# An attention turn in another order: four score tiles, a pair's values in one run, three score tiles

## The chip, the cores and the metric

The kernel runs on one core of a Trainium2 chip. The core has a tensor engine (PE), whose weight loads are a row of their own in the profile (PEld), a vector engine (DVE), a scalar engine (ACT), GpSimd (POOL) and queues that issue DMA transfers (SP among them). Each engine takes its instructions in program order, and semaphores hold an instruction back until what it needs is there. The metric is device microseconds of one execution, the median of several runs.

## The reference

Attention over 4 batches of 12 heads, 448 positions and 64 columns per head, and behind it two gated MLPs over the 1792 tokens that come out:

```python
q_n, k_n = (rmsnorm(q, g_q), rmsnorm(k, g_k))      # each row / its rms, times g
scores = scale * np.matmul(q_n, k_n.transpose(0, 1, 3, 2))
scores = scores - np.max(scores, axis=-1, keepdims=True)
attn = np.exp(scores)
attn = attn / (np.sum(attn, axis=-1, keepdims=True) + 1e-09)
out = np.matmul(attn, v)                           # (4, 12, 448, 64)
x = out.transpose(0, 2, 1, 3).reshape(1792, 768)
x = (x @ w_a * (x @ w_b)) @ w_out                  # 768 -> 1536 -> 768
x = (sigmoid(x @ w_gate) * (x @ w_val)) @ w_out2   # the same sizes
```

All inputs and the result are 32-bit floats.

## The kernel before

Attention takes the 48 heads as 24 pairs; the first 320 us are theirs, and the MLPs behind them are not touched. The two heads of a pair lie in the two halves of the 128 partitions. The 448 positions are 384 (three blocks of 128) and a remainder of 64. For each pair the work goes through these steps, each a small function in the code:

- `load`, `load_r`, `load_v` fetch q and k, the remainder rows of a whole batch, and v. `squares` (POOL), `mean` (DVE), `rsqrt` (ACT), `newton` (DVE) make the factor 1/rms of each row, `scale` (POOL) multiplies by it.
- `t_tr` transposes q (four PE transposes) and k (five); `q_hi`, `k_hi` (ACT) round the result to a short float (QH, KH), `q_lo`, `k_lo` (DVE) keep what the rounding lost (QL, KL).
- `s` makes a score tile as three products, KH by QH, KH by QL, KL by QH. The rows of queries make seven tiles of 128 x 448: tiles t and t+4 belong to the two heads and are made together, in the two row halves of the array (`s(i, 0)`, `s(i, 1)`, `s(i, 2)`, two tiles each); tile 3 holds the remainder queries of both heads and uses the full array. `top` (DVE) takes the row maximum, `exp` (ACT) the exponential with the row sum. Four banks of PSUM hold scores.
- `x_tr` transposes the exponentials back, by blocks j of 128 keys, j = 3 the remainder; `x_out` copies the result from PSUM to SBUF, z = 0 by ACT, z = 1 by DVE. Three banks of PSUM hold what PE transposes, `t_tr` and the row sums included.
- `pv` multiplies values and exponentials, two heads for each block j, the heads in the two column halves of the array. The remainder block uses quarters of the array: 64 rows of a head's keys by 64 columns.
- `rsum`, `rsum_tr`, `rsum_post` turn the sums into reciprocals, transpose them and write them to DRAM (`dr`); `rsum_get` reads them back spread over partitions (`rs`, three DMAs), `norm` (DVE) multiplies `pv` by `rs` into `xs`, and `put` stores it. `early`, `early_hi`, `early_lo` prepare, for six of the last pairs, what the first MLP starts with: `early_lo` is a POOL subtraction over 896 columns.

The order on every engine is written out by hand. `begin`, `turns` and `end` are tables of entries (step, offset, arguments); `turns` runs once for each pair i from 1 to 22, and an entry with offset o works on pair i + o. The program order on each engine is the order in which the entries come. In a turn of the kernel before, the products of values come at four places (`pv(-2, 3)`, `pv(-1, 0)`, `pv(-1, 1)`, `pv(-1, 2)`), and score tiles at four places between transposes.

Of the kernel before, what the change touches and what calls it, by code (L numbers as in the profile page):

```python
# [23 lines left out]
def attention_then_two_gated_mlps(  # L24
# [93 lines left out]
    def attention():  # L118
# [22 lines left out]

        qrem = fx.tile([P, P], F32, name="qrem")
# [40 lines left out]
        def squares(i):  # L183
# [4 lines left out]
            r = rem[i // NP][0][:, :, i % NP]  # L188
# [32 lines left out]
        def scale(i, n):  # L221
# [45 lines left out]
        def k_hi(i):  # L267
            d = st[i]
            KH, KL = (qk.tile([P, S], F32R, tag=n, name=n) for n in ("KH", "KL"))
# [4 lines left out]
            nc.scalar.activation(out=KH, in_=d["T", 1][:, 0:S], func=AF.Copy, scale=G)  # L274
# [5 lines left out]
        def k_lo(i):  # L280
# [3 lines left out]
            nc.vector.scalar_tensor_tensor(out=KL, in0=kt, scalar=G, in1=f32(KH), op0=ALU.mult, op1=ALU.subtract)  # L284

        def s(i, t):
# [18 lines left out]
        def exp(i, t):  # L305
            d = st[i]
            e = pp.tile([P, S], F32, tag="P", name="P")
# [3 lines left out]
            d["P"][t] = e  # L311

        def x_tr(i, j, z):
# [3 lines left out]
            if j < R:  # L317
                if z == 0:
                    out7 = tr.rearrange("p (b x) -> p b x", x=64)[:, 0:8:7, :]
                    nc.tensor.transpose(out7, p[3][:, P * j:P * j + P], ident)  # L320
                o = 0 if z else 64
                for c in range(3):
                    nc.tensor.transpose(tr[:, o + P * c:o + P * c + P], p[4 * z + c][:, P * j:P * j + P], ident)  # L323
                return
            for m, a, perm in ((128, 4, swap), (64, 0, ident)):
                nc.tensor.transpose(tr[0:m, 0:P], p[3][:, S - m:S], perm)
                for c in range(3):
                    nc.tensor.transpose(tr[0:m, 64 + P * c:64 + P * c + P], p[a + c][:, S - m:S], ident)
# [12 lines left out]
        def pv(i, j):  # L341
            d = st[i]
            b, hp = divmod(i, NP)
            if j == 0:
                d["pv"] = ps_v.tile([P, S], F32, tag="pv", name="pv")
            for h in range(2):
                e = slice(64 * h, 64 * h + 64)
                if j < R:
                    w, x = d["v"][:, R * h + j], d["pt"][j][:, S * h:S * h + S]
                else:  # L350
                    w, x = rem[b][1][e, hp], d["pt"][j][e, 0:S]
                nc.tensor.matmul(d["pv"][e], w, x, start=(j == 0), stop=(j == R), skip_group_check=True)  # L352
# [77 lines left out]
        def mlp(i, n):  # L430
# [10 lines left out]
            (exp, 0, 0), (q_lo, 1), (rsqrt, 2), (k_hi, 1), (top, 0, 4), (s, 0, 3), (exp, 0, 4), (newton, 2),
            (squares, 3), (top, 0, 1), (exp, 0, 1), (k_lo, 1), (s, 0, 2), (scale, 2, 1),
            (top, 0, 5), (exp, 0, 5), (top, 0, 3), (exp, 0, 3), (scale, 2, 2), (top, 0, 2),
            (top, 0, 6), (t_tr, 2, 1), (scale, 2, 0), (t_tr, 2, 0), (exp, 0, 2), (mean, 3),
            (s, 1, 0), (load, 4), (k_hi, 2), (k_lo, 2), (top, 1, 0), (q_hi, 2),
            (load_r, 3), (squares, 4), (q_lo, 2), (x_tr, 0, 0, 0),
# [3 lines left out]
            (top, 0, 4), (exp, -1, 6), (rsqrt, 2), (early_hi, -1), (s, 0, 1), (x_tr, -1, 0, 1), (top, 0, 1),  # L450
            (exp, 0, 0), (x_out, -1, 0, 0), (exp, 0, 4), (pv, -2, 3), (load_v, 1), (norm, -2),
            (s, 0, 3), (put, -2), (early_lo, -1), (early, 0), (top, 0, 5), (exp, 0, 1), (newton, 2), (x_tr, -1, 1, 0),
            (x_out, -1, 0, 1), (x_tr, -1, 1, 1), (scale, 2, 1), (top, 0, 3), (x_out, -1, 1, 0),
            (exp, 0, 5), (pv, -1, 0), (s, 0, 2), (x_tr, -1, 2, 0), (scale, 2, 2),
            (rsum, -1), (x_out, -1, 1, 1), (top, 0, 2), (rsum_tr, -1),
            (exp, 0, 3), (scale, 2, 0), (top, 0, 6), (x_tr, -1, 2, 1), (x_out, -1, 2, 0),
            (rsum_post, -1), (exp, 0, 2), (pv, -1, 1), (x_out, -1, 2, 1),
            (load, 4), (load_r, 3), (t_tr, 2, 1), (x_tr, -1, 3, 0), (t_tr, 2, 0),
            (mean, 3), (s, 1, 0), (k_hi, 2), (q_hi, 2), (k_lo, 2), (squares, 4),
            (x_out, -1, 3, 0), (q_lo, 2), (pv, -1, 2), (x_tr, 0, 0, 0), (top, 1, 0),  # L460
            (rsum_get, -1),
# [3 lines left out]
            (exp, -2, 6), (top, -1, 4), (s, -1, 1), (x_tr, -2, 0, 1), (rsum, -2), (exp, -1, 0), (top, -1, 1),  # L465
            (s, -1, 3), (x_out, -2, 0, 0), (exp, -1, 4), (x_out, -2, 0, 1),
            (pv, -3, 3), (exp, -1, 1), (top, -1, 5), (rsum_tr, -2),
            (norm, -3), (x_tr, -2, 1, 0), (top, -1, 3), (rsum_post, -2), (x_tr, -2, 1, 1), (s, -1, 2),
# [7 lines left out]
            (x_tr, -1, 0, 1), (pv, -2, 3), (rsum, -1), (x_out, -1, 1, 0), (x_out, -1, 0, 1), (decode, -1, 4),
            (decode, -1, 5), (decode, -1, 6), (decode, -1, 7),
            (decode, -1, 8), (mlp, -1, 0), (stage, -1, "A21", 0), (rsum_tr, -1), (x_tr, -1, 1, 1), (mlp, -1, 1),
            (rsum_post, -1), (mlp, -1, 2), (x_out, -1, 1, 1), (decode, -1, 9), (norm, -2),
            (mlp, -1, 3), (stage, -1, "A21", 1), (x_tr, -1, 2, 0), (x_tr, -1, 2, 1),  # L480
            (mlp, -1, 4), (pv, -1, 0), (x_out, -1, 2, 0), (x_out, -1, 2, 1), (mlp, -1, 5),
            (mlp, -1, 6), (stage, -1, "A21", 2),
            (pv, -1, 1), (x_tr, -1, 3, 0), (mlp, -1, 7), (x_out, -1, 3, 0), (mlp, -1, 8),
            (rsum_get, -1), (mlp, -1, 9), (pv, -1, 2), (stage, -1, "A11", 0),
            (mlp, -1, 10), (mlp, -1, 11), (put, -2),
            (mlp, -1, 12), (pv, -1, 3), (mlp, -1, 13), (stage, -1, "A11", 1), (norm, -1), (mlp, -1, 14), (put, -1),
# [758 lines left out]
```

## Time and profile before

| | |
|---|---|
| time, median of 3 runs | 1297.03 us (1294.79 to 1297.15) |
| the profiled execution | 1292.24 us |
| its span in the trace | 1290.5 us, so 1.74 us lie around it |
| granted PE clock, mean | 0.989 |
| PE busy in the span | 1241.7 us (96%) |
| DVE, ACT, POOL busy | 938.9 us, 658.0 us, 169.5 us |

The profile is of one execution. Busy time of PE counts a matmul from its start to its modelled end, and matmuls overlap, so the duration in a row of PE is longer than the time until the next row starts; the distance between starts is what a group of matmuls costs. The attention part is the first ten of the forty slices of the span: PE is busy 9 tenths of each slice but the first, POOL 4 or 5 tenths, ACT 6 or 7, DVE 6 or 7.

### The profile page before, as it was taken

To read this page: it belongs to the slowest core of one execution; us is meant where nothing else is said; L and a number is where in the kernel's file an instruction comes from. 1 tells how busy PE (TensorE), PEld (TensorE's weight loads), DVE (VectorE), ACT (ScalarE), POOL (GpSimd) and SP (SyncE) were. 2 spreads that over 40 slices of the span, in tenths; PEclk is the share of its full clock that TensorE was granted. 3 is DMA by queue.
4 is the path that set the end of the run, shared out by engine and by line. 5 is a ranking of instruction groups with operands and counts; after the bars stand their busy time and mean duration, and the time that the engine had idled before them with its cause. 6 is when DMAs were issued, how large, how long until landed. Compare 5 with 4: busy or idle time off the path is not lost.

```text
span 1290.5 us, 18247 instructions
## 1 busy us (share of the span) xinstructions
PE 1241.7 (96%) x6486; PEld 1020.0 (79%) x6486; DVE 938.9 (73%) x1617; ACT 658.0 (51%) x1267; POOL 169.5 (13%) x200
## 2 busy tenths in 40 slices
PE   5999999999979999999999998989999999999997
PEld 3555555555658888888888887878888888899997
DVE  7676767676797778777567688976778777558583
ACT  4666666766454353343444645653454453444543
POOL 4454445540000000000002022000000000000000
PEclk9999999999989999999999999989999999999999
DMA  4333233323914455555486563413556556487573
GB/s 110 88 93 100 80 101 120 120 75 109 312 45 137 139 171 193 165 175 194 147 299 195 169 224 109 139 61 125 173 159 195 165 164 202 157 289 244 179 250 119
DMA packets 142026, 203.01 MB, mean 157 GB/s; under 512 B 23240, under 2 KB 116592, under 8 KB 141936
## 3 DMA queue, kind: packets, MB, share of 16 engines
q1 hardware_dynamic: 140816, 201.27, 48.9%
q8 instruction: 51, 0.84, 0.3%
q10 hardware_dynamic: 1120, 0.59, 0.2%
q14 instruction: 39, 0.32, 0.1%
HBM read 147.46 MB, written 54.35 MB: 156 GB/s over the span
## 4 chain that ended last, share of the span: by engine, by line
PE 59%; DVE 8%; ACT 3%; issue 2%; DMA 1%; ACTq 0%; SPq 0%; DVEq 0%
PE mm L865 41%; PE mm L1127 9%; PE mm L1117 8%; DVE xl L554 2%; DVE wl L554 1%; ACT gh L1034 1%; DVE d L1004 1%; DVE gl L554 1%; DVE al L778 1%; DVE u L1022 0%; DVE d L624 0%; DVE raw L620 0%; DVE u L778 0%; DVE d L700 0%; DMA u<-gd 0%
## 5 line engine op out<-in xcount | busy, mean ns | idle before, releaser
L865 PE MATMUL mm<-xh,wh 128*128 128x512 f32 (+1 forms) x1008 | 371.6, 369 | 11.0 <-ACT u L917 4.1
L865 PE MATMUL mm<-xl,wh 128*128 128x512 f32 (+1 forms) x1008 | 371.8, 369 | 4.7 <-DVE xl L554 4.7
L865 PE MATMUL mm<-xh,wl 128*128 128x512 f32 (+1 forms) x1008 | 372.4, 369 | 0.0
L554 DVE TENSOR_TENSOR wl<-d,wh 128x384 fp32r<-128x384 f32 x252 | 143.7, 571 | 153.7 <-ACT wh L712 93.5
L865 PEld LDWEIGHTS mm<-xh,wh 128*128 128x128 f32 x1008 | 191.4, 190 | 38.9 <-ACT u L917 5.1
L865 PEld LDWEIGHTS mm<-xl,wh 128*128 128x128 f32 x1008 | 191.1, 190 | 30.0 <-DVE xl L554 7.1
L865 PEld LDWEIGHTS mm<-xh,wl 128*128 128x128 f32 x1008 | 191.0, 189 | 21.6 <-DVE wl L554 0.3
L712 ACT CAST wh<-d 128x384 fp32r<-128x384 f32 x168 | 85.9, 512 | 168.1 <-DVE d L700 142.1
L301 DVE TENSOR_REDUCE nm<-s 128x1 f32<-128x448 f32 x168 | 99.8, 618 | 32.1 <-PE s L295 31.9
L1007 ACT CAST wh<-d 128x384 fp32r<-128x384 f32 x84 | 43.2, 514 | 149.9 <-DVE d L1004 54.3
L308 ACT ACTIVATE P<-s,nm 128x448 f32<-128x448 f32 x168 | 106.6, 636 | 15.9 <-DVE nm L301 15.1
L617 ACT ACTIVATE d<-raw 128x384 f32<-128x384 f32 x136 | 75.8, 558 | 72.9 <-DMA raw<-in_moe_w_gate_dram 15.0
L1127 PE MATMUL mm<-wh,gh 128*128 128x384 f32 x294 | 98.8, 336 | 0.5 <-ACT ah L1150 0.3
L1127 PE MATMUL mm<-wl,gh 128*128 128x384 f32 x294 | 98.6, 335 | 0.0
L1127 PE MATMUL mm<-wh,gl 128*128 128x384 f32 x294 | 98.5, 335 | 0.0
L1117 PE MATMUL mm<-gh,wh 128*128 128x512 f32 x252 | 92.5, 367 | 5.1 <-ACT ah L1150 4.4
L1117 PE MATMUL mm<-gl,wh 128*128 128x512 f32 x252 | 93.2, 370 | 0.0
L1117 PE MATMUL mm<-gh,wl 128*128 128x512 f32 x252 | 93.0, 369 | 0.0
L352 PE MATMUL pv<-pt,v 128*64 128x448 f32 x288 | 87.2, 564 | 5.7 <-DVE pt L337 4.8
L554 DVE TENSOR_TENSOR gl<-u,gh 128x896 fp32r<-128x896 f32 x60 | 71.3, 1188 | 18.4 <-ACT gh L1034 18.3
L624 DVE SCALAR_TENSOR_TENSOR d<-d,raw 128x384 uint32<-128x384 uint32 x136 | 75.8, 557 | 10.8 <-DVE raw L620 0.4
L339 ACT COPY pt<-tr 128x512 f32<-128x512 f32 x96 | 54.7, 571 | 51.6 <-PE tr L323 47.9
(145 smaller groups left out, 1975.8 us busy)
## 6 DMA issues: line engine op xcount, KB each, us to landing
gd<-u SPq DMA_DIRECT2D x60, 448.0 KB
u<-gd SPq DMA_DIRECT2D x60, 448.0 KB
d<-wd SPq DMA_DIRECT2D x132, 192.0 KB
raw<-in_moe_w_out_dram SPq DMA_DIRECT2D x48, 384.0 KB
wd<-d SPq DMA_DIRECT2D x72, 192.0 KB
raw<-in_moe_w_val_dram SPq DMA_DIRECT2D x23, 384.0 KB
raw<-in_moe_w_a_dram SPq DMA_DIRECT2D x22, 384.0 KB
raw<-in_moe_w_b_dram SPq DMA_DIRECT2D x22, 384.0 KB
```

The source lines that it names most:

```text
L301: nc.vector.tensor_reduce(out=d["nm"][:, t:t + 1], in_=d["ps"][t], axis=AX.X, op=ALU.max, negate=True)
L308: nc.scalar.activation(out=e, in_=d["ps"].pop(t), func=AF.Exp, bias=d["nm"][:, t:t + 1], accum_out=d["sum"][:, t:t + 1])
L339: nc.scalar.copy(out=d["pt"][j][:, w], in_=tr)
L352: nc.tensor.matmul(d["pv"][e], w, x, start=(j == 0), stop=(j == R), skip_group_check=True)
L554: eng.tensor_tensor(out=lo, in0=t, in1=f32(hi), op=ALU.subtract)
L617: nc.scalar.activation(out=f32(t), in_=f32(high), func=AF.Copy, scale=2.0 ** -112)
L624: nc.vector.scalar_tensor_tensor(out=t, in0=t, scalar=3, in1=low, op0=ALU.logical_shift_left, op1=ALU.bitwise_or)
L712: nc.scalar.copy(out=hi, in_=t)
L865: nc.tensor.matmul(ps[:, o:o + size], w[:, P * c:P * c + P], x[:, o:o + size], start=(p in (1, 5) and c == 0 and z == 0), stop=(c == KC - ...
L1007: nc.scalar.copy(out=hi, in_=t)
L1117: nc.tensor.matmul(ps[:, o:o + size], w[:, P * un:P * un + P], g[:, o:o + size], start=(p in (1, 5) and f == 0 and z == 0), stop=(f == HF ...
L1127: nc.tensor.matmul(ps[:, o:o + HB], g[:, P * t:P * t + P], w, start=(p in (1, 5) and f == 0 and z == 0), stop=(f == HF - 1 and z == 2), sk ...
```

## The change

The change does five things to the attention part, and nothing to the MLPs.

First, the order of a turn. The three places with two score tiles and the place with one become two: `s(0)`, `s(1)` (four tiles) at the head of a turn, and `s(2)`, `s(3)` (three tiles) after the values. `pv` makes all eight products of a pair in one run. All transposes stand in two long rows, one behind each group of scores. The pipeline is deeper: values and the last transposes belong to pair i-2, the result of `put` to pair i-3; and `rsum_get` stands at the head of a turn, a turn behind `rsum_post`.

Second, the values of the remainder rows lie in two tiles `rz` that POOL zero-fills once. A head's values stand in its own half of the rows, the other half is zero, so that the product of block 3 takes 128 rows as the other blocks do.

Third, tiles t and t+4 of the exponentials share one tile of 896 columns. The last 64 keys of the first head then lie beside the first 64 key columns of the second head. A new step `k_ends` rotates the second head's keys by 64: POOL copies its last 64 columns to the front of KH and of KL, two copies of 64x64 for each pair. One transpose of 128 columns then serves both heads, and `x_tr(i, 3, 0)` has five transposes in place of eight.

Fourth, buffers: `pp` has 8 tiles of 896 columns and 3 of 448 in place of 13 of 448, `pt` 4 and 2 in place of 3, `vv` 3 in place of 4.

Fifth, `begin` and `end` are written anew to fit.

```diff
@@ load_r, and its zero-filled tiles
+        rz = [fx.tile([P, 2, NP, D], F32, name=f"rz{i}") for i in range(2)]
+        for t in rz:
+            nc.gpsimd.memset(t, 0.0)
-                out=rem[b][0][64 * h:64 * h + 64, n] if n < 2 else rem[b][1][64 * h:64 * h + 64],
+                out=rem[b][e, n] if n < 2 else rz[b % 2][e, h],
@@ keys
-            KH, KL = (qk.tile([P, S], F32R, tag=n, name=n) for n in ("KH", "KL"))
+            KH, KL = (qk.tile([P, 512], F32R, tag=n, name=n) for n in ("KH", "KL"))
-            nc.scalar.activation(out=KH, in_=d["T", 1][:, 0:S], func=AF.Copy, scale=G)
+            nc.scalar.activation(out=KH[:, 64:512], in_=d["T", 1][:, 0:S], func=AF.Copy, scale=G)
+        def k_ends(i):
+            for x in st[i]["K"]:
+                nc.gpsimd.tensor_copy(x[64:128, 0:64], x[64:128, 448:512])
@@ scores
-            parts = [(3, slice(0, P))] if t == 3 else [(t, slice(0, 64)), (t + 4, slice(64, P))]
+            parts = [(3, slice(0, P), 64)] if t == 3 else [(t, slice(0, 64), 64), (t + 4, slice(64, P), 0)]
-                    nc.tensor.matmul(out_, w[e, o:o + P], x[e, :], start=(n == 0), stop=(n == 2))
+                    nc.tensor.matmul(out_, w[e, o:o + P], x[e, m:m + S], start=(n == 0), stop=(n == 2))
@@ x_tr, remainder keys
-            for m, a, perm in ((128, 4, swap), (64, 0, ident)):
-                nc.tensor.transpose(tr[0:m, 0:P], p[3][:, S - m:S], perm)
-                for c in range(3):
-                    nc.tensor.transpose(tr[0:m, 64 + P * c:64 + P * c + P], p[a + c][:, S - m:S], ident)
+            nc.tensor.transpose(tr[:, 0:P], p[3][:, S - P:S], swap)
+            nc.tensor.transpose(tr[0:64, 0:P], p[3][:, NQ:S], ident)
+            for c in range(3):
+                nc.tensor.transpose(tr[:, 64 + P * c:64 + P * c + P], p[c][:, NQ:NQ + P], ident)
@@ pv
-        def pv(i, j):
+        def pv(i):
+            for j in range(R + 1):
+                for h in range(2):
-                    w, x = rem[b][1][e, hp], d["pt"][j][e, 0:S]
+                        w, x = rz[b % 2][:, h, hp], d["pt"][j][:, 0:S]
@@ turns (the first rows of the table)
-            (top, 0, 4), (exp, -1, 6), (rsqrt, 2), (early_hi, -1), (s, 0, 1), (x_tr, -1, 0, 1), (top, 0, 1),
+            (rsum_get, -2), (early, 0), (s, 0, 0), (exp, -1, 3), (rsqrt, 2), (s, 0, 1), (x_tr, -2, 2, 1), (newton, 2),
```

The order of a turn on PE before, from its second score tile pair on. In these rows s is a score tile, tr a transpose into PSUM, pv a product of values, and xN counts instructions alike:

```order
L295 MATMUL s<-KH,QH 128x448 x2
L295 MATMUL s<-KH,QL 128x448 x2
L295 MATMUL s<-KL,QH 128x448 x2
L352 MATMUL pv<-pt,v 64x448 x2
L320 MATMUL tr<-ident,P 128x2x64
L323 MATMUL tr<-ident,P 128x128 x3
L295 MATMUL s<-KH,QH 128x448 x2
L295 MATMUL s<-KH,QL 128x448 x2
L295 MATMUL s<-KL,QH 128x448 x2
L323 MATMUL tr<-ident,P 128x128 x3
L352 MATMUL pv<-pt,rv 64x448 x2
```

Here a product of values or a few transposes stand between any two score tiles.

The middle of a turn on PE after, from the values on, P_626 being tile 3 of the exponentials and rc the reciprocals of the row sums:

```order
L364 MATMUL pv<-pt,v 64x448 x6
L364 MATMUL pv<-pt,rz_281 64x448 x2
L305 MATMUL s<-KH,QH 128x448 x2
L305 MATMUL s<-KH,QL 128x448 x2
L305 MATMUL s<-KL,QH 128x448 x2
L305 MATMUL s<-KH,QH 128x448
L305 MATMUL s<-KH,QL 128x448
L305 MATMUL s<-KL,QH 128x448
L333 MATMUL tr<-ident,P_626 128x2x64
L336 MATMUL tr<-ident,P 128x128 x6
L378 MATMUL tr<-ident,rc 7x128
```

The eight products are one run, the three score tiles follow it, and the transposes begin behind these.

The same place one turn later with what each instruction waits for, down to the next pair's first scores (P_789 is tile 3 of that pair; _49 is part of the semaphores' names):

```order
L378 MATMUL tr<-ident,rc 7x128 [waits DVE_49,PE_49]
L333 MATMUL tr<-ident,P_789 128x2x64 [waits Activation_49]
L336 MATMUL tr<-ident,P 128x128 x3
L336 MATMUL tr<-ident,P 128x128 [waits DVE_49]
L336 MATMUL tr<-ident,P 128x128 x2
L333 MATMUL tr<-ident,P_789 128x2x64 [waits DVE_49]
L336 MATMUL tr<-ident,P 128x128 x3
L305 MATMUL s<-KH,QH 128x448
L305 MATMUL s<-KH,QH 128x448 [waits Activation_49,Pool_49]
L305 MATMUL s<-KH,QL 128x448 x2
```

What moved: nineteen transposes and the row sums' one now stand together, three groups of them wait for the copy that empties a bank (ACT or DVE), and the second head's first product waits for ACT and for POOL's copy of the keys.

ACT in the same stretch after; row is the copy of the transposed reciprocals:

```order
L352 COPY pt<-tr 128x512
L323 ACTIVATE P,sum<-s,nm 128x448 x2
L352 COPY pt<-tr 128x512
L383 COPY row<-tr 7x128
L352 COPY pt<-tr 128x512
L323 ACTIVATE P_954,sum<-s,nm 128x448
L211 ACTIVATE y<-ms 128x14
```

The exponential of tile 3 (P_954) stands behind the last of the three copies, and the square root's first part (L211) behind both.

## Rows read from the trace of the kernel before

**Rows 1.** One turn: us, busy PE PEld DVE ACT POOL, PEclk, DMA share, GB/s

```profile
100.59:113.04 12.45, 12.45 (x78) 7.13 (x77) 8.66 (x21) 8.34 (x23) 5.91 (x8) 1.00 0.32 95
```

**Rows 2.** PE in that turn, in time order: start us, us, engine, operation

```profile
101.39 0.97 PE L352 MATMUL pv<-pt,v 128*64 128x448 f32 x4
102.29 0.33 PE L320 MATMUL tr<-ident,P 128*128 128x128 f32 x1
...
102.88 0.47 PE L295 MATMUL s<-KH,QH 64*128 64x448 f32 x2
...
103.68 0.55 PE L323 MATMUL tr<-ident,P 128*128 128x128 f32 x3
...
106.62 1.76 PE L352 MATMUL pv<-pt,v 128*64 128x448 f32 x4
108.31 0.47 PE L295 MATMUL s<-KH,QH 64*128 64x448 f32 x2
...
111.03 0.55 PE L249 MATMUL tr<-ident,qkn 128*128 128x128 f32 x3
...
113.04 0.47 PE L295 MATMUL s<-KH,QH 64*128 64x448 f32 x2
```

**Rows 3.** ACT in time order, the same turn

```profile
102.22 0.22 ACT L209 ACTIVATE y<-ms 128x14 f32<-128x14 f32 x1
...
106.40 0.59 ACT L339 COPY pt<-tr 128x512 f32<-128x512 f32 x1 [1.23 <-PE tr L323]
106.88 0.64 ACT L308 ACTIVATE P<-s,nm 128x448 f32<-128x448 f32 x1
107.41 0.20 ACT L308 ACTIVATION_READ_ACCUMULATOR P<-s,nm 128x1 f32 x1
...
111.84 0.64 ACT L274 ACTIVATE KH<-tr,G 128x448 fp32r<-128x448 f32 x1 [0.68 <-PE tr L255]
```

**Rows 4.** DVE in time order, the same turn

```profile
106.31 0.17 DVE L217 SCALAR_TENSOR_TENSOR t<-y 128x14 f32<-128x14 f32 x1
...
106.81 0.55 DVE L337 COPY pt<-tr 128x384 f32<-128x384 f32 x1
107.27 0.61 DVE L301 TENSOR_REDUCE nm<-s 128x1 f32<-128x448 f32 x1
...
110.75 0.61 DVE L201 TENSOR_REDUCE ms<-sq 128x14 f32<-128x448 f32 x1
...
112.51 0.68 DVE L284 SCALAR_TENSOR_TENSOR KL<-tr,G,KH 128x448 fp32r<-128x448 f32 x1 [0.94 <-ACT KH L274]
```

**Rows 5.** POOL in time order, the same turn

```profile
108.26 0.98 POOL L241 TENSOR_SCALAR qrem<-rqk,y 64x64 f32<-64x64 f32 x2
```

**Rows 6.** PE starts: pairs 3, 22, 23, and the first MLP matmul

```profile
50.96 0.47 PE L295 MATMUL s<-KH,QH 64*128 64x448 f32 x2
...
293.61 0.47 PE L295 MATMUL s<-KH,QH 64*128 64x448 f32 x2
...
304.53 0.47 PE L295 MATMUL s<-KH,QH 64*128 64x448 f32 x2
...
319.00 0.50 PE L865 MATMUL mm<-xh,wh 128*128 128x512 f32 x1
```

**Rows 7.** Table of waits, 30 to 330 us: total us, times, longest

```profile
DVE xs L385 <- DMA rs<-dr: 5.7, 4, 2.2
```

**Rows 8.** DVE, then POOL, in the turn of pair 15

```profile
206.55 0.62 DVE L385 TENSOR_TENSOR xs<-pv,rs 128x448 f32<-128x448 f32 x1 [2.24 <-DMA rs<-dr]
...
207.62 1.54 DVE L217 SCALAR_TENSOR_TENSOR t<-y 128x14 f32<-128x14 f32 x1
...
207.06 2.07 POOL L413 TENSOR_TENSOR xl<-xst,xh 128x896 fp32r<-128x896 f32 x1
```

**Rows 9.** Two windows ahead of and in a fall of the clock

```profile
360.00:365.00 5.00, 2.31 (x12) 1.89 (x11) 5.00 (x7) 3.43 (x6) 0.00 (x0) 1.00 0.00 0
365.00:375.60 10.60, 7.87 (x20) 5.84 (x21) 10.31 (x16) 4.54 (x8) 0.00 (x0) 0.52 0.30 99
```

More of the change, by code (lines that the diff above doesn't have):

```diff
@@ L241, in scale, with ends @@
                 eng.tensor_scalar(out=dst, in0=r[e, n], scalar1=y[e, n, 6:7], scalar2=None, op0=ALU.mult)
+        def ends(t):
+            return t.rearrange("p (b x) -> p b x", x=64)[:, 0:8:7, :]
         def t_tr(i, n):
@@ L306, in exp @@
             d = st[i]
-            e = pp.tile([P, S], F32, tag="P", name="P")
+            if t == 3:
+                e = d["P"][t] = pp.tile([P, S], F32, tag="P3", name="P3", bufs=3)
+            else:
+                if t < 4:
+                    d["P"][t] = pp.tile([P, S2], F32, tag="P", name="P")
+                e = d["P"][t % 4][:, S * (t // 4):S * (t // 4) + S]
             nc.scalar.activation(
@@ L332, in x_out @@
             if z == 0:
-                d["pt"][j] = pt.tile([P, S2], F32, tag="pt", name="pt", bufs=3)
+                d["pt"][j] = pt.tile([P, S if j == R else S2], F32, tag=f"pt{j == R}", name="pt", bufs=2 if j == R else 4)
             w = slice(0, S) if j == R else slice(512 * z, S2 if z else 512)
@@ L339, in x_out @@
                 nc.scalar.copy(out=d["pt"][j][:, w], in_=tr)
-        def pv(i, j):
+        def pv(i):
             d = st[i]
             b, hp = divmod(i, NP)
[L344 to L350, printed above, removed]
-                    w, x = rem[b][1][e, hp], d["pt"][j][e, 0:S]
-                nc.tensor.matmul(d["pv"][e], w, x, start=(j == 0), stop=(j == R), skip_group_check=True)
+            d["pv"] = ps_v.tile([P, S], F32, tag="pv", name="pv")
+            for j in range(R + 1):
+                for h in range(2):
+                    if j < R:
+                        w, x = d["v"][:, R * h + j], d["pt"][j][:, S * h:S * h + S]
+                    else:
+                        w, x = rz[b % 2][:, h, hp], d["pt"][j][:, 0:S]
+                    nc.tensor.matmul(
+                        d["pv"][64 * h:64 * h + 64], w, x, start=(j == 0), stop=(j == R), skip_group_check=True
+                    )
         def rsum(i):
@@ L437, in attention @@
             (load_r, -1), (scale, 0, 0), (load_r, 0), (scale, 0, 2), (t_tr, 0, 1), (k_hi, 0), (squares, 1),
-            (mean, 1), (t_tr, 0, 0), (rsqrt, 1), (load_v, 1), (k_lo, 0), (newton, 1), (load, 3), (load_r, 1),
+            (mean, 1), (t_tr, 0, 0), (rsqrt, 1), (k_lo, 0), (k_ends, 0), (newton, 1), (load, 3), (load_r, 1),
             (q_hi, 0), (q_lo, 0), (scale, 1, 1), (load_r, 2), (s, 0, 0), (scale, 1, 0), (scale, 1, 2),
-            (t_tr, 1, 0), (top, 0, 0), (load_v, 0), (s, 0, 1), (squares, 2), (q_hi, 1), (mean, 2), (t_tr, 1, 1),
@@ L441, in attention @@
[L441 to L446, printed above, removed]
+            (s, 0, 1), (top, 0, 0), (load_v, 0), (load_v, 1), (t_tr, 1, 0), (squares, 2), (exp, 0, 0), (top, 0, 4), (q_hi, 1),
@@ L447, in attention @@
+            (mean, 2), (t_tr, 1, 1), (exp, 0, 4), (q_lo, 1), (rsqrt, 2), (k_hi, 1), (top, 0, 1), (newton, 2),
+            (exp, 0, 1), (top, 0, 5), (scale, 2, 1), (k_lo, 1), (k_ends, 1), (exp, 0, 5), (s, 0, 2), (s, 0, 3), (load, 4),
+            (scale, 2, 0), (scale, 2, 2), (top, 0, 2), (load_r, 3), (exp, 0, 2), (top, 0, 6), (squares, 3),
+            (exp, 0, 6), (top, 0, 3), (mean, 3),
         )
         turns = (
-            (top, 0, 4), (exp, -1, 6), (rsqrt, 2), (early_hi, -1), (s, 0, 1), (x_tr, -1, 0, 1), (top, 0, 1),
@@ L451, in attention @@
[L451 to L461, printed above, removed]
+            (rsum_get, -2), (early, 0), (s, 0, 0), (exp, -1, 3), (rsqrt, 2), (s, 0, 1), (x_tr, -2, 2, 1), (newton, 2),
+            (top, 0, 0), (exp, 0, 0), (x_out, -2, 2, 1), (x_tr, -2, 3, 0), (top, 0, 4), (x_out, -2, 3, 0), (exp, 0, 4),
@@ new lines, in attention @@
+            (t_tr, 1, 1), (top, 0, 1), (k_hi, 1), (k_lo, 1), (exp, 0, 1), (t_tr, 1, 0), (q_hi, 1), (top, 0, 5),
+            (q_lo, 1), (pv, -2), (exp, 0, 5), (k_ends, 1), (scale, 2, 1), (scale, 2, 0), (scale, 2, 2), (squares, 3), (load, 4),
+            (load_r, 3), (put, -3), (load_v, 1), (rsum, -1), (early_hi, -1), (early_lo, -1), (s, 0, 2), (s, 0, 3),
+            (norm, -2), (x_tr, -1, 0, 0), (top, 0, 2), (x_out, -1, 0, 0), (exp, 0, 2), (x_tr, -1, 0, 1), (top, 0, 6),
+            (x_out, -1, 0, 1), (rsum_tr, -1), (x_tr, -1, 1, 0), (exp, 0, 6), (x_out, -1, 1, 0), (rsum_post, -1),
@@ L462, in attention @@
+            (top, 0, 3), (x_tr, -1, 1, 1), (x_out, -1, 1, 1), (x_tr, -1, 2, 0), (mean, 3), (x_out, -1, 2, 0),
         )
         end = (
[L465 to L468, printed above, removed]
@@ L476, in attention @@
[L476 to L481, printed above, removed]
@@ L482, in attention @@
[L482 to L486, printed above, removed]
-            (mlp, -1, 15), (stage, -1, "A11", 2),
+            (rsum_get, -3), (s, -1, 0), (exp, -2, 3), (s, -1, 1), (x_tr, -3, 2, 1), (top, -1, 0), (exp, -1, 0),
@@ new lines, in attention @@
+            (x_out, -3, 2, 1), (x_tr, -3, 3, 0), (top, -1, 4), (x_out, -3, 3, 0), (exp, -1, 4), (top, -1, 1),
+            (exp, -1, 1), (top, -1, 5), (x_tr, -2, 0, 0), (rsum, -2), (pv, -3), (exp, -1, 5), (x_out, -2, 0, 0),
+            (put, -4), (s, -1, 2), (s, -1, 3), (norm, -3), (x_tr, -2, 0, 1), (top, -1, 2), (x_out, -2, 0, 1),
+            (exp, -1, 2), (rsum_tr, -2), (x_tr, -2, 1, 0), (top, -1, 6), (x_out, -2, 1, 0), (rsum_post, -2),
+            (exp, -1, 6), (top, -1, 3), (x_tr, -2, 1, 1), (x_out, -2, 1, 1), (put, -3), (x_tr, -2, 2, 0),
```

50 lines of the change are left out of this document (26 added, 24 removed).

## The prediction

> **What bounds the kernel now.** I read the busy times of one plain turn first, then PE in time order through it, then ACT, DVE and POOL in the same stretch, then the starts of the pairs, and last the table of waits. A plain turn lasts 12.45 us, and in it PE is busy all 12.45, at a granted clock of 1.00, DVE 8.66, ACT 8.34, POOL 5.91 [rows 1]. So PE sets the turn; the reader is to see that its groups follow each other without a hole [rows 2]. Two things in PE's time are not work. A group of four transposes takes 0.59 us (102.29 to 102.88) though in a long row of 17 they take 2.01 (111.03 to 113.04): with 0.15 at the head of a group the rest is 0.11 for each. The same 0.15 stands at the head of every group of another kind: two score tiles 0.80, one pair of value products 0.90 [rows 2]. A turn has twelve such heads. And one pair of groups of values takes 1.69 instead of 0.90 (106.62 to 108.31): 0.79 in which PE stands in a matmul and DVE's copy, which ends at 107.36, is what the second half needs [rows 2, 4].
>
> Pairs 3 to 22 take 19 turns, 293.61 - 50.96 = 242.65 us [rows 6]. At 12.45 that is 236.55; 6.1 are more. They have two causes. DVE waited 5.7 us for the reciprocals that come back from DRAM, four times, 2.2 the longest [rows 7], and a wait of that length shows in PE's turn, since the next row maxima stand behind `norm` on DVE [rows 8]. In six turns POOL's `early_lo` takes 2.07 us, and DVE's `newton` beside it 1.54 instead of 0.17 [rows 4, 8], so 1.37 more on an engine with room. I give the first 4.0 of the 6.1 and the second 2.1.
>
> GpSimd's slow subtraction beside DVE is what the Trainium skill's "GPSIMD Engine Reference", section 8, Key points, says of the two engines: they share SBUF interfaces, and a DVE instruction with two SBUF inputs collides. The trace agrees (0.17 against 1.54); by that rule the two new copies of `k_ends` could slow such DVE instructions too, by at most their own length.
>
> **The change, part by part.** PE's own work first. Three transposes go: 3 x 0.11 = 0.33. Twelve heads become five (four score tiles, 17 transposes, values, two score tiles, tile 3 with 19 transposes): 7 x 0.15 = 1.05. The stall of 0.79 goes, because the values of pair i-2 were copied a turn before. The zero-filled remainder product has the same 448 columns. 12.45 - 0.33 - 1.05 - 0.79 = 10.28 us. That would be the turn if nothing else came last, and I don't think it is: two rings come out longer.
>
> The first ring runs through PE and the copies that empty the transposes' three banks. Now 19 transposes stand in one row and each group but the first ones needs a bank back; before, scores and values stood between them and hid the copies. From the values on, in us: eight products, 4 x 0.75 + 0.15 = 3.15; three score tiles 0.80 and about 0.70 (between 0.60 without a head and 0.80); the first four transposes until ACT has them 0.64; ACT's copy 0.59 and 0.05 until PE goes on; seven transposes 0.15 + 0.77 + 0.05, about 1.0; DVE's copy 0.55 and 0.05, since the next group takes that bank; four transposes 0.64; ACT's copy 0.48 until the exponential behind it begins (106.40 to 106.88); the exponential of tile 3 with its sum 0.73 (106.88 to 107.61) and 0.05, since the second of the next pair's score tiles needs its bank; those scores 0.80; 17 transposes 2.01 [rows 2 to 4]. Sum: 3.15 + 1.50 + 0.64 + 0.64 + 1.00 + 0.60 + 0.64 + 0.48 + 0.78 + 0.80 + 2.01 = 12.24.
>
> The second ring runs through POOL, whose work is one row now: `k_ends`, the three steps of `scale`, `squares`. `k_ends` needs KL, and the next KL needs DVE behind `newton`, which needs `squares`. POOL's present work is 5.91 busy and about 0.25 between [rows 1]; about 0.25 more to cross from KL to POOL and on; `mean` 0.61 and a short one behind, 0.8; `rsqrt` two of 0.22; `newton` 0.50 (106.31 to 106.81) and 0.06 between; a row maximum about 0.55, a copy 0.46, a maximum 0.61 on DVE; an exponential 0.64; KH 0.64; KL 0.68 [rows 3, 4]. That is 11.8, and one copy of `k_ends` is added, since the copy of KH can go while KL is made. The trace has no such copy. The nearest row is POOL's two instructions on 64x64, 0.98 for both [rows 5], so 0.49 for one; at that 12.3. From below 0.2 (12.0), POOL being given a simpler instruction; from above both copies behind KL, 0.98 (12.8).
>
> Two rings of nearly the same length on engines that they share: I take 12.30 for a turn, 0.15 less than now. Nineteen turns: 233.7. The six turns with `early_lo` keep their 2.1, since POOL does it behind `squares` and ahead of the `newton` that waits for the same. Of the waits for reciprocals 1.0 of 4.0 is kept: the three reads now stand on SP directly behind the write of the row, at the head of a turn, and `norm` comes behind the values, some 8 us later (3.15 of values, 2.01 of transposes and two groups of scores lie between), while SP's loads of q, k and v are queued behind the reads and not ahead of them. What comes late instead would be the loads, which have two turns. 233.7 + 2.1 + 1.0 = 236.8 against 242.65: -5.85.
>
> The ends give some back. Pair 22's turn lasts 304.53 - 293.61 = 10.92 now, since no later pair's q and k are transposed in it [rows 6]; after, that turn still has the nine of pair 23 and stays a full one: +1.4. From pair 23's first score to the first matmul of the MLP are 319.00 - 304.53 = 14.47 [rows 6]. After, the same stretch holds about the same work on PE (43 transposes 4.7, values 6.0, scores 2.4, heads about 1.2: 14.3), but with its transposes in a row as in a turn, where the first ring is 2 us longer than PE's work: between 0 and +2, +1.0 taken, as decoding for the MLP stands between. The beginning: two zero-fills of 768 columns on POOL (some 1.2 us each, by ACT's 0.59 for 512 columns) at a time when POOL is not needed, and pair 0's seven score tiles together, but a deeper pipeline to fill: between -1.5 and +2, +0.5 taken. Sum: -5.85 + 1.4 + 1.0 + 0.5 = -2.95. The profiled execution has 1292.24, 4.8 below the median shown; so 1289.3 in its terms, and 1297.03 - 2.95, about 1294.0, as a median.
>
> **The rivals.** *No ring, PE's own work decides* (or nearly): if the copies keep ahead of the transposes, a turn falls to 12.0 or less; 19 turns at 12.0 and no stall left are 230.1, -12.5, with the ends -9.6: 1287.4. At 10.28 it would be 38 us, near 1258; against it stand the waits for ACT and DVE that the new order has in its row of transposes. *The turn does not get shorter*: 12.45 again, because the rings lengthen each other, with the reciprocals' waits gone all the same: 19 x 12.45 + 2.1 + 1.0 = 239.65, -3.0, with +2.9 at the ends: 1297.
>
> *Slower, by POOL's ring.* If both copies of `k_ends` stand behind KL and cost 0.98 together, a turn is 12.8: 243.2 + 2.1 + 1.0 = 246.3, +3.65, and +2.9 at the ends: 1303.6. It decides from about 0.8 for the copies on (12.6, where the gain from the stalls is used up). For it speaks that POOL takes 0.49 for one instruction of 64 columns [rows 5], against it that KH is ready 0.7 before KL.
>
> *Slower, by the clock.* The granted clock fell to 0.52 for 10.6 us behind a stretch in which PE was busy 2.31 of 5.00 us [rows 9]; in the turn shown it holds 1.00, through 2.01 us of transposes alone too [rows 1, 2]. After, a stretch of about 4 us has transposes alone with waits between. A fall like the one shown would halve PE's rate for 10.6 us: 10.28 of 12.3 are work, so 8.9 would take 17.8 against 10.6 there, some 5 lost net of the waits that it fills. Two falls would be +10 - 3 = +7: 1304; one in each turn far more. The Trainium skill has a rule that speaks for it: "TensorE: Matmul & The Clock Gate", Part 4: PE-mode transpose, says that transposes don't count as PE activity as other matmuls do. No row here shows it: the clock did not fall in the 2.01 us.
>
> **How the numbers follow.** The forecast (turn 12.3) has a chance of 0.46, with its own range 1290 to 1298 from the bounds of the ends, the stalls and the first copy; about half of it lies beyond 0.2% (2.6 us), which is what a measurement of this kernel can tell from no change. PE's work nearer to deciding 0.18, the turn not shorter 0.13, POOL's ring 0.15, the clock 0.08. Faster by over 0.2%: 0.25 + 0.18 + 0.02 = 0.45. Slower: 0.14 + 0.08 and 0.04 from the two cases around no change, 0.26. Within: 0.29. The range 1284 to 1303 leaves out the far part of PE's case and most of the clock's and some of POOL's.
>
> **What would show it.** PE's order with heads gone: about 36 transposes in a turn, values in 3.1 us, and idle time of PE of some 2 us in each turn, released by ACT's and DVE's copies of `pt` and by the exponential of tile 3. Pairs 12.3 apart. No wait of `norm` for reciprocals. The copies on POOL at 0.2 to 0.5. A granted clock of 1.00 in the attention. I am wrong where pairs are 12.0 or 12.8 apart, where the first MLP matmul comes over 3 us later against pair 22 than now (25.4 us), or where the clock shows falls.

## The result and the profile after

The changed kernel takes 1307.14 us (median of 4 runs, 1306.09 to 1307.58) against 1295.91 us for the kernel before (4 runs): a ratio of 1.0088, 95% interval 1.007 to 1.0106. It is slower by about 11 us; 1294.0 was forecast, and the time lies outside the range. The profiled executions are 1307.06 and 1292.24 us, 14.8 apart: the one of before is 3.7 below its median, so some 3 to 4 us of what the two traces differ by is its scatter. One of the four executions of the kernel with three edits further down took 3484 us and is left out of its numbers.

The starts of pairs 2, 3, 22 and 23 and of the MLP in the profile after, as in [rows 6]:

```profile
40.70 0.48 PE L305 MATMUL s<-KH,QH 64*128 64x448 f32 x2
...
53.47 0.47 PE L305 MATMUL s<-KH,QH 64*128 64x448 f32 x2
...
293.96 0.47 PE L305 MATMUL s<-KH,QH 64*128 64x448 f32 x2
...
306.33 0.47 PE L305 MATMUL s<-KH,QH 64*128 64x448 f32 x2
...
323.89 0.48 PE L867 MATMUL mm<-xh,wh 128*128 128x512 f32 x1
```

Pair 3 starts 2.5 us later than before, the 19 turns to pair 22 take 240.5 instead of 242.65 (2.2 gained), and from there to the first MLP matmul 29.9 instead of 25.4 (4.5 lost). The rest is behind that: the 301st MLP matmul comes 94.25 us after the first, before it was 84.68. That is 9.6 lost in a stretch whose MLP steps the change leaves as they are; but the table `end`, which sets the last pairs' steps between them, was written anew. 0.3 more comes later.

A plain turn after, first as a window (columns as in [rows 1]), then PE in time order:

```profile
127.62:139.98 12.36, 11.17 (x74) 7.08 (x73) 8.94 (x20) 8.08 (x23) 6.35 (x11) 1.00 0.31 85
```

```profile
127.62 0.47 PE L305 MATMUL s<-KH,QH 64*128 64x448 f32 x2
...
128.99 0.47 PE L305 MATMUL s<-KH,QH 64*128 64x448 f32 x1 [0.29 <-ACT P L323]
...
129.79 0.55 PE L336 MATMUL tr<-ident,P 128*128 128x128 f32 x3
...
131.80 2.48 PE L364 MATMUL pv<-pt,v 128*64 128x448 f32 x12
...
134.96 0.48 PE L305 MATMUL s<-KH,QH 64*128 64x448 f32 x2
...
136.48 0.28 PE L333 MATMUL tr<-ident,P 128*128 128x128 f32 x1
...
137.76 0.33 PE L333 MATMUL tr<-ident,P 128*128 128x128 f32 x1 [0.24 <-ACT pt L352]
...
139.40 0.33 PE L333 MATMUL tr<-ident,P 128*128 128x128 f32 x1 [0.65 <-DVE pt L350]
...
139.98 0.47 PE L305 MATMUL s<-KH,QH 64*128 64x448 f32 x2
```

The turn is 12.36. PE is no longer busy throughout: it stands at three places in brackets, for ACT's copy, for DVE's copy and for the exponential of tile 3. The values take 3.16 (131.80 to 134.96); the prediction had summed 3.15.

In the six turns with `early_lo` pairs are 13.1 to 13.4 apart. DVE and POOL in one of them:

```profile
227.51 0.62 DVE L203 TENSOR_REDUCE ms<-sq 128x14 f32<-128x448 f32 x1 [0.93 <-POOL sq L196]
228.16 1.40 DVE L204 TENSOR_SCALAR ms<-ms 128x14 f32<-128x14 f32 x1
230.15 0.17 DVE L219 SCALAR_TENSOR_TENSOR t<-y 128x14 f32<-128x14 f32 x1 [0.59 <-ACT y L212]
```

```profile
226.35 1.13 POOL L196 TENSOR_TENSOR sq<-sq 128x448 f32<-128x448 f32 x1
227.44 2.10 POOL L427 TENSOR_TENSOR xl<-xst,xh 128x896 fp32r<-128x896 f32 x1
233.75 0.24 POOL L294 CAST KH<-KH 64x64 fp32r<-64x64 f32 x1 [4.21 <-ACT KH L278]
234.40 0.24 POOL L294 CAST KL<-KL 64x64 fp32r<-64x64 f32 x1 [0.41 <-DVE KL L288]
```

The second instruction of `mean`, 0.17 in a plain turn (128.34), takes 1.40 beside POOL's subtraction. In the order before it was `newton` that stood there [rows 8]. The copies of `k_ends` take 0.24 each.

At the hand-over, DVE's two last `norm`, PE behind the first, and SP's queue ahead of it:

```profile
329.06 0.63 DVE L399 TENSOR_TENSOR xs<-pv,rs 128x448 f32<-128x448 f32 x1 [3.40 <-DMA rs<-dr]
...
341.46 0.62 DVE L399 TENSOR_TENSOR xs<-pv,rs 128x448 f32<-128x448 f32 x1 [5.78 <-PE pv L364]
```

```profile
331.41 0.33 PE L338 MATMUL tr<-swap,P 128*128 128x128 f32 x1 [2.59 <-DVE pt L350]
```

```profile
318.92 0.49 SPq L608 DMA_DIRECT2D u<-in_moe_w_a_dram  x1
322.94 0.37 SPq L608 DMA_DIRECT2D raw<-in_moe_w_b_dram  x1
323.41 1.73 SPq L392 DMA_DIRECT2D rs<-dr  x3
```

The three reads of pair 22's reciprocals stand in SP's queue behind a fifth load of weights, which waits from 319.4 to 322.9 for its buffer. So `norm` holds DVE for 3.4 us; the copies of transposes and the decoding of weights are queued behind it; PE waits. The last `norm` holds DVE 5.8 us until PE has made the last values. Between 330 and 340 us the granted clock is 0.66 in the mean: from 332.16 to 338.99 it is 0.50, the lower of its two levels (1.2 of 2.4 GHz), else 1.00:

```profile
330.00:340.00 10.00, 7.06 (x24) 3.91 (x26) 4.97 (x11) 3.65 (x7) 0.00 (x0) 0.66 0.83 264
```

The same place in the kernel before, SP's queue and then the last two `norm`:

```profile
316.30 0.37 SPq L606 DMA_DIRECT2D raw<-in_moe_w_b_dram  x1
316.77 1.73 SPq L378 DMA_DIRECT2D rs<-dr  x3
```

```profile
323.33 0.62 DVE L385 TENSOR_TENSOR xs<-pv,rs 128x448 f32<-128x448 f32 x1
...
336.62 0.63 DVE L385 TENSOR_TENSOR xs<-pv,rs 128x448 f32<-128x448 f32 x1 [4.23 <-PE pv L352]
```

The reads stood behind the fifth load there too. But `norm` of pair 22 came behind the first three MLP steps, where it now comes ahead of them, and found its reciprocals there. The last `norm` waited as well, 4.2 us; it stood behind MLP step 13 and now stands behind step 7. So what is new is where the table `end` has the two `norm`, and how late the reads are: 0.5 us ahead of the first MLP matmul, before it was 2.2.

### The profile page after: what moved, and what is told of

The parts are those of the page before. It is cut to its first block, busy times and chain, and to the rows that moved or that the text cites. A ratio compares the mean times of both kernels' runs of the same rounds, so it can differ in the third digit from the quotient of the medians.

```text
span 1305.2 us, 18186 instructions
## 1 busy us (share of the span) xinstructions
PE 1223.7 (94%) x6414; PEld 1026.1 (79%) x6414; DVE 947.1 (73%) x1617; ACT 654.5 (50%) x1267; POOL 181.6 (14%) x250
## 4 chain that ended last, share of the span: by engine, by line
PE 58%; DVE 7%; ACT 3%; issue 2%; DMA 1%; ACTq 0%; SPq 0%; DVEq 0%
PE mm L867 42%; PE mm L1129 9%; PE mm L1119 8%; DVE xl L556 1%; ACT gh L1036 1%; DVE d L1006 1%; DVE gl L556 1%; DVE wl L556 1%; DVE u L1024 1%; DVE al L780 1%; ACT xh L771 0%; DVE d L626 0%; ACT ah L1156 0%; DVE u L780 0%; DMA d<-wd 0%
## 5 line engine op out<-in xcount | busy, mean ns | idle before, releaser
L619 ACT ACTIVATE d<-raw 128x384 f32<-128x384 f32 x136 | 75.7, 558 | 73.5 <-DMA raw<-in_moe_w_a_dram 16.5
L622 DVE SCALAR_TENSOR_TENSOR raw<-raw 128x384 uint32<-128x384 uint32 x136 | 76.0, 559 | 4.0
```

Source lines behind the costliest of these rows:

```text
L619: nc.scalar.activation(out=f32(t), in_=f32(high), func=AF.Copy, scale=2.0 ** -112)
L622: nc.vector.scalar_tensor_tensor(out=low, in0=high, scalar=0x80000000, in1=low, op0=ALU.bitwise_and, op1=ALU.bitwise_or)
```

## The experiments

Three theories stood against each other in the first four runs. (A ring is a chain of steps that comes round once a turn, each waiting for the one before, so that its length bounds the turn from below.) R: a ring through `squares` on POOL, `mean`, `newton`, the row maxima, the keys and `scale` makes turns long. B: the ring of the transposes' banks does. T: the loss behind the attention is made by DVE's waits in the last table, and not by weights that come late.

**The factor late.** `mean`, `rsqrt` and `newton` moved from the ends of the turn to behind the keys (`begin` loses its `mean` of pair 3 too; cuts are marked by ...):

```diff
-            (rsum_get, -2), (early, 0), (s, 0, 0), (exp, -1, 3), (rsqrt, 2), (s, 0, 1), (x_tr, -2, 2, 1), (newton, 2),
+            (rsum_get, -2), (early, 0), (s, 0, 0), (exp, -1, 3), (s, 0, 1), (x_tr, -2, 2, 1),
-            (t_tr, 1, 1), (top, 0, 1), (k_hi, 1), (k_lo, 1), (exp, 0, 1), (t_tr, 1, 0), ...
-            (q_lo, 1), (pv, -2), ...
+            (t_tr, 1, 1), (top, 0, 1), (k_hi, 1), (mean, 2), (k_lo, 1), (exp, 0, 1), (rsqrt, 2), (t_tr, 1, 0), ...
+            (newton, 2), (q_lo, 1), (pv, -2), ...
-            (top, 0, 3), (x_tr, -1, 1, 1), (x_out, -1, 1, 1), (x_tr, -1, 2, 0), (mean, 3), (x_out, -1, 2, 0),
+            (top, 0, 3), (x_tr, -1, 1, 1), (x_out, -1, 1, 1), (x_tr, -1, 2, 0), (x_out, -1, 2, 0),
```

> The changed kernel with mean, root and newton of a pair moved behind the keys' KL on DVE and ACT, so that the next row maxima no longer stand behind squares on POOL. Theory R (the ring squares - mean - newton - row maxima - KH - KL - k_ends - scale - squares sets the turn): plain pairs 12.36 now, about 12.25 apart after (the transposes' banks are next); the six pairs with early_lo, 13.35 now, also below 12.6; pair 2, at 40.70 now, 2 to 4 us earlier; in all 8 to 12 us, about 1297. Rival B (the transposes' banks set it): plain pairs stay 12.36, the six stay above 13, within 2 us of 1307. Rival P (POOL is slowed or too full): the six stay above 13.

Measured: 1297.58 us (10 runs), ratio to before 1.0007, 95% interval 0.9998 to 1.0017. Starts of pair 2 and of two of the six pairs:

```profile
37.01 0.47 PE L305 MATMUL s<-KH,QH 64*128 64x448 f32 x2
...
222.39 0.47 PE L305 MATMUL s<-KH,QH 64*128 64x448 f32 x2
...
234.75 0.47 PE L305 MATMUL s<-KH,QH 64*128 64x448 f32 x2
```

Pair 2 comes 3.7 us earlier and the six turns are 12.36: in the beginning and in the six, the factor's ring had set the pace. But plain turns stayed exactly 12.36. Of them theory R is wrong, and what B forecast came true; of the six and of the time it did not.

**`early_lo` ahead.** One edit to the changed kernel: the two steps moved behind `newton`, where POOL is idle.

```diff
-            (load_r, 3), (put, -3), (load_v, 1), (rsum, -1), (early_hi, -1), (early_lo, -1), (s, 0, 2), (s, 0, 3),
+            (load_r, 3), (put, -3), (load_v, 1), (rsum, -1), (s, 0, 2), (s, 0, 3),
-            ... (x_tr, -2, 2, 1), (newton, 2),
+            ... (x_tr, -2, 2, 1), (newton, 2), (early_hi, -1), (early_lo, -1),
```

> The changed kernel with early_hi and early_lo moved to the head of the turn, behind newton, where POOL waits for KH (5.3 us idle in a plain turn). Theory R (in the six turns early_lo stands beside mean and its second DVE instruction, which it stretches, inside the ring): the six pairs 12.4 apart instead of 13.35, about -6 us. Rival P (2.1 us more for POOL cost the same wherever they stand): the six stay at 13.2 or more.

Measured: 1299.68 us in one run; POOL and DVE there:

```profile
229.10 2.10 POOL L427 TENSOR_TENSOR xl<-xst,xh 128x896 fp32r<-128x896 f32 x1 [2.55 <-ACT xh L421]
```

```profile
226.59 0.62 DVE L203 TENSOR_REDUCE ms<-sq 128x14 f32<-128x448 f32 x1 [0.70 <-POOL sq L196]
227.24 0.17 DVE L204 TENSOR_SCALAR ms<-ms 128x14 f32<-128x14 f32 x1
```

POOL's 2.1 us are the same, the instruction of `mean` is back at 0.17, and the six turns are 12.36 (226.52 to 238.88). It was what stood beside the subtraction that cost 1 us in each of six turns, not POOL's load.

**The reads early, the last `norm` late.** Two edits to the last table `end`, each alone, and both together with the factor late:

```diff
-            ... (close, -1), (exp, -1, 3), (decode, -1, 0), (decode, -1, 1), ...
-            (rsum_get, -2), (x_tr, -1, 0, 0), ...
+            ... (close, -1), (exp, -1, 3), (decode, -1, 0), (rsum_get, -2), (decode, -1, 1), ...
+            (x_tr, -1, 0, 0), ...
```

```diff
-            (mlp, -1, 7), (pv, -1), (stage, -1, "A11", 0), (norm, -1), (put, -1),
+            (mlp, -1, 7), (pv, -1), (stage, -1, "A11", 0),
-            ... (mlp, -1, 13), (stage, -1, "A11", 1),
+            ... (mlp, -1, 13), (stage, -1, "A11", 1), (norm, -1), (put, -1),
```

> The changed kernel with the reads of pair 22's reciprocals issued in the last table directly behind the first four weight loads, not behind the fifth. Theory T (norm holds DVE for 3.4 us at 325.7, the copies of the last transposes stand behind it, PE and the weights' decoding wait): that wait goes, and the 37th matmul of the MLP comes 3 to 5 us earlier against the first; no low clock between 332 and 341. Rival W (the weights themselves come late, since their loads are issued 6 us later than before): the wait goes but the 37th matmul stays as far from the first as now (21.6 us), within 1 us.

> The changed kernel with one edit: norm and put of the last pair moved in the last table behind four more MLP steps. Theory N (the last norm holds DVE for 5.8 us at 335.7 until PE has made the values, and the decoding of weights stands behind it; that is the second part of the late hand-over): the wait goes, and the 301st matmul of the MLP comes 3.5 to 6 us earlier against the first (94.25 us now), about 1302. Rival (the reads' wait of 3.4 us before it makes all of the lateness): within 1 us of 94.25.

> The changed kernel with the edits of the first and the third run together, and with the last pair's norm moved in the last table behind four more MLP steps, so that DVE does not wait 5.8 us for values. Theory R and T: 1307 - 10 - 4 - 4, about 1288 to 1291, below the kernel before (1296). If the hand-over to the MLP depends on something else (weights, clock): 1295 or more.

Measured, from the first MLP matmul to the 37th and to the 301st, in us:

| kernel | time | 37th | 301st |
|---|---|---|---|
| before | 1295.9 | 15.7 | 84.7 |
| changed | 1307.1 | 21.6 | 94.2 |
| factor late, `end` as changed | 1297.6 | 20.4 | 92.2 |
| `early_lo` ahead, `end` as changed | 1299.7 (one run) | 20.7 | 92.3 |
| reads early | 1303.7 (one run) | 16.5 | 90.1 |
| last `norm` late | 1302.4 (one run) | 20.5 | 89.1 |
| both, and the factor late | 1288.2 (3 runs) | 15.5 | 84.6 |

`norm` in the run with the reads early, and in the one with all three edits:

```profile
326.07 0.62 DVE L399 TENSOR_TENSOR xs<-pv,rs 128x448 f32<-128x448 f32 x1
...
336.88 0.62 DVE L399 TENSOR_TENSOR xs<-pv,rs 128x448 f32<-128x448 f32 x1 [4.17 <-DMA rs<-dr]
```

```profile
316.04 0.62 DVE L399 TENSOR_TENSOR xs<-pv,rs 128x448 f32<-128x448 f32 x1
...
326.43 0.63 DVE L399 TENSOR_TENSOR xs<-pv,rs 128x448 f32<-128x448 f32 x1 [0.35 <-PE pv L364]
```

With the reads early the 37th matmul comes 5.0 us earlier, which weights that come late would not have let it: theory T came true. The edits are worth 4.1 and 5.2 us alone; with the factor late besides, all 9.7 that had been lost behind the first MLP matmul are back. But 2 of these came with the factor late alone, and with `early_lo` ahead alone, both with the changed kernel's `end`: against them the two edits are worth 7.6. Whether those 2 us hang on when the hand-over begins or are scatter of one trace is not shown. Each edit leaves a wait: with the reads early the last `norm` still waits 4.17, which the trace puts down to its own reads; with the last `norm` late it still waits 2.39 for the values. Putting `norm` of pair 22 back behind the MLP steps was not run.

With the reads early the clock is 1.00 between 330 and 340 us, though the weights' loads are issued as late as in the changed kernel:

```profile
330.00:340.00 10.00, 7.62 (x36) 4.21 (x34) 4.66 (x10) 3.50 (x8) 0.00 (x0) 1.00 0.80 263
```

The wait of 2.59 that PE had for DVE's copy of the transposes is gone there. In the three other runs that keep it (1.9 to 2.1 us) the clock falls at that place too, in the run with all three edits it doesn't: the fall came with that wait. The three edits give 0.9936 of the time before, interval 0.9917 to 0.9955.

**The banks' ring.** Two steps on the kernel with all three edits. First, the first half of block 2's transposes is put behind the next pair's scores, and the exponential of tile 3 from there to the end of its own turn (`begin` and `end` follow). Then that exponential is put ahead of a copy as well:

```diff
-            ... (early, 0), (s, 0, 0), (exp, -1, 3), (s, 0, 1), (x_tr, -2, 2, 1),
+            ... (early, 0), (s, 0, 0), (s, 0, 1), (x_tr, -2, 2, 0), (x_out, -2, 2, 0), (x_tr, -2, 2, 1),
-            (top, 0, 3), (x_tr, -1, 1, 1), (x_out, -1, 1, 1), (x_tr, -1, 2, 0), (x_out, -1, 2, 0),
+            (top, 0, 3), (x_tr, -1, 1, 1), (x_out, -1, 1, 1), (exp, 0, 3),
```

```diff
-            ... (x_tr, -1, 1, 0), (exp, 0, 6), (x_out, -1, 1, 0), (rsum_post, -1),
-            (top, 0, 3), (x_tr, -1, 1, 1), (x_out, -1, 1, 1), (exp, 0, 3),
+            ... (x_tr, -1, 1, 0), (exp, 0, 6), (top, 0, 3), (exp, 0, 3), (x_out, -1, 1, 0), (rsum_post, -1),
+            (x_tr, -1, 1, 1), (x_out, -1, 1, 1),
```

> The fourth run's kernel with the four transposes of block 2, first half, taken from the end of the second row of transposes and put behind the next pair's first four score tiles, and the exponential of tile 3 now ahead of their copy. Theory B (what sets 12.36 in a plain turn is the ring of the transposes' banks: values 3.16, scores 1.52, 0.64, copy 0.64, 1.02, DVE's copy 0.62, 0.69, copy 0.48, exponential 0.78, scores 0.80, transposes 2.01): DVE's copy and one group drop out of it, pairs 11.6 to 11.8 apart, about -14 us against 1288.7. Rival: PE's row with its waits is not what sets the turn (the factor's ring or the exponentials on ACT do): pairs stay above 12.2.

> As the run before, and the exponential of tile 3 with its maximum ahead of ACT's copy of block 1, so that the next pair's second score tiles find their bank free. Theory B: its 0.48 and 0.78 drop out too, pairs 11.0 to 11.2 apart, about 1261 to 1266. Rival: ACT's or DVE's own load (8.3 to 8.9 a turn) with its order sets in first: 11.6 or more, 1273 or more.

Measured: 1275.92 us in one run, pairs 11.75 apart (106.21 to 117.96); then 1263.12 us (4 runs), ratio to before 0.9755, interval 0.9729 to 0.9781, pairs 11.15 apart. The second kernel's turn, as a window and as PE's rows:

```profile
113.97:125.12 11.15, 10.91 (x75) 7.08 (x74) 9.14 (x20) 7.87 (x24) 6.36 (x11) 1.00 0.21 58
```

```profile
124.20 0.33 PE L333 MATMUL tr<-ident,P 128*128 128x128 f32 x1 [0.24 <-ACT pt L352]
124.37 0.82 PE L336 MATMUL tr<-ident,P 128*128 128x128 f32 x6
125.12 0.48 PE L305 MATMUL s<-KH,QH 64*128 64x448 f32 x2
```

PE has one wait of 0.24 left, and is busy 10.91 of 11.15. The two steps shortened the turn by 0.61 and 0.60, as expected, and less than the links that went (0.62 and 0.69, then 0.48 and 0.78): the transposes moved still cost PE their time, and at 11.15 PE's own work nearly fills the turn. This version is faster than both kernels, by 32.5 us than before.

**The factor first again, and three transposes more.** On that kernel, `mean`, `rsqrt`, `newton` back where the changed kernel has them; and, apart from it, the remainder's transposes made eight:

```diff
-                nc.tensor.transpose(tr[:, 64 + P * c:64 + P * c + P], p[c][:, NQ:NQ + P], ident)
+                for _ in range(2):
+                    nc.tensor.transpose(tr[:, 64 + P * c:64 + P * c + P], p[c][:, NQ:NQ + P], ident)
```

> The kernel of the run before with mean, root and newton put back to where the changed kernel has them. Theory R (the ring squares - mean - newton - row maxima - keys - scale is a second one, a little under the banks' 12.36): plain pairs 11.9 to 12.1, the six with early_lo 13 or more, pair 2 some 3 us later. Rival: the factor's ring is far shorter than the banks': plain pairs within 0.1 of the run before.

> The sixth run's kernel with three of the five transposes of the remainder keys made twice, so eight again as in the kernel before. If PE's own time lies on the turn's ring in this order: pairs 0.33 farther apart (3 x 0.11), some 7.5 us more. If the row has slack at the copies: 0.1 or less.

Measured in one run each: 1293.37 us, plain pairs 12.15 apart (113.30 to 125.45), a little above the 11.9 to 12.1 expected, four of the six 13.3 to 13.4 (the others 15.0 and 11.7), pair 2 at 40.00 instead of 36.10; and 1269.79 us, pairs 11.39 apart (105.40 to 116.79). So the factor's ring was a second one, 0.2 under the banks' 12.36, and either alone takes most of what the new order can gain. Three transposes are worth 0.24 in this order, less than 3 x 0.11. PE's one wait is 0.24 with them and without, so it does not make up the rest, and what does is not shown.

## Why the prediction was wrong

The sum was -2.95 us; the two profiled executions differ by +14.8 (the medians by +11.2, so that some of what follows is scatter). By its own terms:

- *The turn.* The forecast was 12.30, the banks' ring being 12.24 by hand. Measured 12.36, with the waits where the ring had them, and the two runs that took links out showed it to be the cause. The mechanism was right and the size 0.06 short, 1.1 us in 19 turns. The step from PE's work to a longer ring was the useful one: PE's busy time did fall (11.17), and 1.2 of the 1.3 gained was given back as waits. But the work itself was put too low, at 10.28: with one wait of 0.24 left PE was still busy 10.91. So the rival that let a turn fall to 10.28 was priced too low (by its own sum it would be about 1255, not 1258).
- *The six turns with `early_lo`* failed: "The six turns with `early_lo` keep their 2.1, since POOL does it behind `squares` and ahead of the `newton` that waits for the same." It is true that it stands there. But in the new order what it stretches lies on the factor's ring, and that ring was only 0.2 under the other: 13 turns at 12.36, the six about 1 more each, 5.7 instead of 2.1. The moved `early_lo` showed it. The 2.1 was too small for the kernel before as well: nearly all of the 6.1 us that its 19 turns have over 12.45 lie in these six, which take 80.73 (200.49 to 281.22), 6.0 more than six plain ones. One wait for reciprocals of 2.24 is in that [rows 8], so 3.8 or more is left for `early_lo`; beside it `newton` took 0.56 to 0.60 four times, 1.54 once, and once 2.03 (at 272.62), in a turn of 14.29. The six turns after take 79.84: they did not get longer, they missed the gain.
- *The waits for reciprocals.* In the turns they went, all of them; the 1.0 kept was not needed. The waits table has the only one left, 3.4 us, in the last table.
- *The ends.* The beginning lost 2.5 instead of 0.5: pair 0's seven score tiles come early, but pair 1's maxima stand behind a `newton` that waits for `squares` of pair 3; moving the factor gave it back. The way from pair 22 to the first MLP matmul lost 4.5 against 2.4, over the 3 that the prediction gave as a sign of being wrong, and the last table's edits did not recover it (30.2 with three edits): 1.4 is the full turn of pair 22. The other 3.1 lie between pair 23's first score and the MLP, 17.56 after. PE's starts there (306.33 to 323.89) give 3.8 to scores, 7.6 to values and 6.2 to transposes, where the prediction summed 2.4, 6.0, 4.7 and 1.2 for heads, 14.3. Of the 3.3 more, 1.0 is in three waits of PE; the rest is work put too low.
- *The step that failed most* is one that the sum does not have: it ends at the first MLP matmul, as if what follows only moved along with it. In the last table attention and MLP share DVE, SP and PE, and 9.6 us were lost there. The prediction asked what is queued behind `rsum_get` on SP in a turn, and did not ask it for the last pairs, where the fifth load of weights stands ahead of the reads and `norm` now comes before they are back, nor for the last `norm`, behind which DVE's decoding stands. The two edits to the last table gave back most of it, with the factor late all; 2 of the 9.6 stay without a cause.

Summed: 1.1 + 3.6 - 1.0 for the 19 turns, 2.0 at the beginning, 2.1 ahead of the MLP, 9.6 in it and 0.3 later are 17.7, which is what lies between -2.95 and +14.8.

Of the rivals, POOL's ring was named with the wrong price: the copies are 0.24 each, not 0.49. With 0.24 the prediction's own sum for that ring is 12.04; alone it measured 12.15. The clock did not fall in the turns, though transposes and their waits fill 3.5 us (136.48 to 139.98) in each; the Trainium skill's rule in "TensorE: Matmul & The Clock Gate", Part 4: PE-mode transpose, that they don't count as activity, is not shown by any run here. It fell at the hand-over, to 0.50, behind PE's wait of 2.59.

## What to carry to other kernels

Work saved on the busiest engine is worth what the next ring leaves of it: write down the ring through the buffers that are emptied by other engines, link by link, before believing the saving, and move the links apart. Where two parts of a program overlap, read the seam as its own stage: for each in-order queue there, ask what stands behind an instruction that can wait, a `norm` on DVE or a read behind a load. A wait that the old order hid can come out when its place among the other part's steps moves. A slow instruction beside another engine's is cheap or dear by what stands beside it, so a reorder has to be read at the rare turns too.

## What was not expected of the hardware

A DVE instruction with one small input (128x14, 0.17 us) took 1.40 beside POOL's subtraction of 896 columns, and 0.17 again when the subtraction was moved away. In the version with the exponential of tile 3 early the first instruction of `rsum` on DVE, 0.19 in the changed kernel, took 0.52 beside POOL's `scale`, to the end of an instruction of POOL's (121.12 to 121.96):

```profile
121.47 0.52 DVE L371 TENSOR_SCALAR rc<-sum 128x7 f32<-128x7 f32 x1
```

So not only instructions with two inputs are held. The Trainium skill's "GPSIMD Engine Reference", section 8, Key points, names two cases, two SBUF inputs or a perf mode that uses both ports; by it this would be the second, and no run here shows which mode the instruction was in. POOL's copy of 64x64 took 0.24, half of its multiplication of the same size [rows 5].
